# Seventeen gathered tiles and two fetched, fetches six blocks ahead, tokens scaled by ScalarE

## The chip, the cores and the metric

The kernel runs on one core of one Trainium2 chip. The metric is the time of one execution in device microseconds, as the median of several runs.

## The reference

A graph of N = 10000 nodes with 160000 edges (src, dst, both drawn at random) carries a 128-wide feature row per node. Seven hops each multiply the features by the normalized adjacency matrix; the eight stages of a node are its tokens, over which a small attention block and a readout run.

```python
h = x                                   # (10000, 128) f32
toks = [x]
for _ in range(7):
    msg = h[src] * deg_inv_sqrt[src, None] * deg_inv_sqrt[dst, None]
    h = segment_sum(msg, dst, N)
    toks.append(h)
tok = stack(toks, axis=1)               # (N, 8, D)
# layernorm, one self-attention over the 8 tokens, residual,
# layernorm, softmax readout over the 8 tokens -> (N, D)
```

## The kernel before

**Tables.** The features of a hop stand in SBUF as a table `tab` of 79 blocks of 128 nodes, 256 f16 wide: 128 columns of the rounded value and 128 of what rounding left over. A copy lies in DRAM (`tabd`), and of its last blocks, from block 4 * NG on, a second copy (`tabh`).

**Slots.** Source and destination blocks are paired. For each of the 78 full destination blocks (NW) and each source block there are 32 slots (CAP) for edges. Four source blocks share a *slot tile* of 128 slots. NG = 18 such tiles are *gathered*: four matmuls with a one-hot matrix of 128 x 32 each (`w`, its second part, fp8) bring the source rows of 4 x 32 slots from `tab` into a PSUM tile `p` (two slot tiles to a buffer, six buffers), ScalarE or VectorE copies `p` to an f16 tile `eb`, and one matmul with a one-hot matrix of 128 x 128 (`w`, its first part) scatters the slots to the 128 destinations in `acc`. The sources from block 72 on are cut into four cells by the constant CELL, which share NI = 1 slot tile that is *fetched*: an indirect DMA issued by GpSimd brings its 128 rows from `tabh` into a tile `og`, and one matmul scatters them. Edges that found no slot go into one more fetched tile, the *over* tile, from `tabd`, with its one-hot matrix `Sov`. The last, partial block is done apart (`ogt`, `end_block`).

**Closing a block.** VectorE adds the two halves of `acc` to `s`; `next_rows` scales `s` into the next table and stores it to `tabd` (and `tabh`) by SP's queue; `token_out` scales `s` into `r`, on GpSimd, and stores it by SP's queue to `tok`.

**Stages.** Pass A sorts the edges (to about 411 us). Hop 1 runs beside the building of the matrices `w`, for four blocks at a time (`place`, `left_out`, `matrices`), and each `w` goes to DRAM (`gsd`). The framework orders the instructions there. Hops 2 to 7 (`later`, `one`) are in an order written by hand: the blocks from 4 * NG on come first, then the others; SP loads `w` some three blocks ahead into five buffers. Within a block PE runs all its gathers, then the fetched tiles, then the scatters but for the last two pairs, which run after the gathers of the next block (`lag`). The close of a hop's first block is held back to the end of the second, and its over tile comes last, as does that of the second block, because over tiles may name any row and so wait for the whole table of the hop before.

**Fetches.** In hops 2 to 7 `ahead(k, n, ...)` runs behind the first eviction of block n and issues the fetches of block n + 2. `mark` first has GpSimd copy one or two columns of the new `eb` into the `og` tile. GpSimd's queue is in order, so all its later work stands behind that eviction.

Of the kernel before, what the change touches and what calls it, by code (L numbers as in the profile page):

```python
# [22 lines left out]
NG = 18  # L23
NI = 1
CELL = 334
# [5 lines left out]
CAP = 32  # L31
NJ = NG + NI
NS = 4 * NJ
# [4 lines left out]
NE = 3  # L38
BIG = 32768.0
# [4 lines left out]
class Hops:  # L44
    def __init__(self, ctx, dp, missing, tab1, tc, x, src, dst, dis):
# [37 lines left out]
        self.zero16 = cp.tile([128, 512], F16, name="zero16")  # L83
# [33 lines left out]
        self.held = []  # L117
# [111 lines left out]
    def lag(self, ep, pp, key, w, a, m):  # L229
# [5 lines left out]
        for b, r, e in parts:  # L235
            T.matmul(W[:, b, :(e - r) * m], self.id16, self.zero16[:, :(e - r) * m], start=True, stop=False, skip_group_check=True)
# [8 lines left out]
    def lag_rows(self, ep, pp, key, w, m):  # L245
# [6 lines left out]
        for b, r, e in parts:  # L252
            T.matmul(W[:, b, :e - r], self.id16, self.zero16[:, :e - r], start=True, stop=False, skip_group_check=True)
# [344 lines left out]
    def mark(self, o, after):  # L598

        if after is not None:  # L600
            self.nc.gpsimd.tensor_copy(o, after.to_broadcast(list(o.shape)))  # L601

    def fetch_end(self, k, src, after=None):
        self.mark(self.ogt[:, k, 0:1], after)
# [3 lines left out]
    def end_block(self, first, fin):  # L608
        m = 257 if first else 256
        acc = self.pacc.tile([128, 512], F32, name="acc", tag="acc")  # L610
        for k in range(NE):
            self.nc.tensor.matmul(acc[:, :m], self.Sov[:, NW + k, :], self.ogt[:, k, :m], start=k == 0, stop=k == NE - 1)
# [7 lines left out]
    def block(self, t, w, tab, og, pend, lag, runs, first, evac, fin, lead=False, late=False, mid=None, ahead=None):  # L620

        nc, V, A, T, G = self.nc, self.nc.vector, self.nc.scalar, self.nc.tensor, self.nc.gpsimd
        m = 257 if first else 256
        acc = []


        def fetched(i, start=False, stop=False):
            W = w[:, (NG + i) * 128:(NG + i + 1) * 128] if i < NI else self.Sov[:, t, :]  # L630
            T.matmul(acc[0][:, :256], W, og()[i], start=start, stop=stop)
            if first:
                T.matmul(acc[0][:, 256:257], W, self.ones16, start=False, stop=False)

        def begin():
            acc.append(self.pacc.tile([128, 512], F32, name="acc", tag="acc"))
            for i in range(NI if late else NI + 1):
                fetched(i, start=i == 0)

        def scat(e, jj):  # L640
            if not acc:
                acc.append(self.pacc.tile([128, 512], F32, name="acc", tag="acc"))
            for j in range(e.shape[1]):
                J = 2 * jj + j
                T.matmul(acc[0][:, :m], w[:, J * 128:(J + 1) * 128], e[:, j, :m], start=first and J == 0,  # L645
                         stop=J == NG - 1 and not (first or late))
                if first and J == 0 and not lead:
# [3 lines left out]
        def close():  # L651
            if first:
                if lead:
                    for i in range(NI):
                        fetched(i)
                T.matmul(acc[0][:, 256:257], self.Sov[:, t, :], self.ones16, start=False, stop=False)
            if first or late:
                T.matmul(acc[0][:, :256], self.Sov[:, t, :], og()[NI], start=False, stop=True)  # L658
            self.finish(t, acc[0], fin)

        def gather(jj):
            n = min(2, NG - 2 * jj)
            p = self.pg.tile([128, 2, 2, 128], F32, name="p")
            for j in range(n):
                for q in range(4):
                    s = 4 * (2 * jj + j) + q
# [847 lines left out]
```

## Time and profile before

| | us |
|---|---|
| runs | 3860.93, 3868.25, 3875.58 |
| median | 3868.25 |
| profiled execution, own time | 3870.73 |
| its span, first to last instruction | 3868.9 |
| pass A and decode | 0 to about 411 |
| hop 1 with the matrices | about 427 to 1117 |
| hops 2 to 7 | 1125 to 3187, each 342 to 345 |
| attention and readout | 3187 to 3869 |

In the profile a line such as "L897 PE MATMUL p<-tab,w ... x33696 | 1008.7, 273" gives line, engine, operation, the tile written and those read, the count, the busy time in us and the mean of one in ns; what follows the second bar is the engine's idle time just before and what ended it. PE is TensorE's matmuls, PEld its weight loads, DVE VectorE, ACT ScalarE, POOL GpSimd, SP the engine whose queue issues plain DMAs. Matmuls overlap, so the spacing of their starts tells more than the duration of one.

### The profile page before, as it was taken

To read this page: it belongs to the slowest core of one execution; us is meant where nothing else is said; L and a number is where in the kernel's file an instruction comes from. 1 tells how busy PE (TensorE), PEld (TensorE's weight loads), DVE (VectorE), ACT (ScalarE), POOL (GpSimd) and SP (SyncE) were. 2 spreads that over 40 slices of the span, in tenths; PEclk is the share of its full clock that TensorE was granted. 3 is DMA by queue.
4 is the path that set the end of the run, shared out by engine and by line. 5 is a ranking of instruction groups with operands and counts; after the bars stand their busy time and mean duration, and the time that the engine had idled before them with its cause. 6 is when DMAs were issued, how large, how long until landed. Compare 5 with 4: busy or idle time off the path is not lost.

```text
span 3868.9 us, 165983 instructions
## 1 busy us (share of the span) xinstructions
PE 3608.5 (93%) x69042; PEld 3019.7 (78%) x69042; DVE 2995.5 (77%) x6973; ACT 2743.1 (71%) x6934; POOL 1844.0 (48%) x2493
## 2 busy tenths in 40 slices
PE   5776899999979999999999999999999999999996
PEld 4665677777768888888888888888888887888885
DVE  8999898888867766766666766676665557999998
ACT  6775477777746666666666666666666669888884
POOL 0000254444446666666666666666666652222222
PEclk8888999999989999999999999999999999999998
DMA  2100354455546666666666666676677541222220
GB/s 91 50 1 1 124 185 163 166 175 177 172 138 207 202 201 202 204 200 200 206 202 204 201 204 201 199 207 202 201 212 212 186 160 48 76 76 76 76 76 24
DMA packets 320888, 590.64 MB, mean 153 GB/s; under 512 B 56780, under 2 KB 214698, under 8 KB 314874
## 3 DMA queue, kind: packets, MB, share of 16 engines
q1 hardware_dynamic: 281945, 501.79, 41.1%
q0 software_dynamic: 35616, 73.01, 7.9%
q8 instruction: 542, 8.88, 0.9%
q10 hardware_dynamic: 2560, 5.12, 0.5%
q14 instruction: 225, 1.84, 0.1%
HBM read 451.66 MB, written 128.06 MB: 150 GB/s over the span
## 4 chain that ended last, share of the span: by engine, by line
PE 71%; DVE 13%; issue 7%; POOL 4%; DMA 3%; ACT 2%; SPq 0%; POOLq 0%; DVEq 0%; ACTq 0%
PE p L897 20%; PE acc L885 19%; PE pv L1174 4%; PE po L1185 3%; PE pu L1163 3%; PE acc L880 3%; POOL og L591 2%; PE acc L645 2%; PE ta L341 2%; PE p L667 2%; PE pt L1153 2%; PE tm L420 2%; POOL r L703 1%; DVE ro L337 1%; DVE R L210 1%
## 5 line engine op out<-in xcount | busy, mean ns | idle before, releaser
L902 ACT CAST eb<-p 128x512 f16<-128x512 f32 x2808 | 1420.4, 602 | 649.4 <-PE p L897 646.3
L902 DVE CAST eb<-p 128x512 f16<-128x512 f32 x1404 | 946.4, 688 | 625.5 <-PE p L897 624.4
L897 PE MATMUL p<-tab,w 128*32 128x256 f16 x33696 | 1008.7, 273 | 5.4 <-DMA w<-gsd 4.6
L885 PE MATMUL acc<-eb,w 128*128 128x256 f16 x8424 | 997.7, 273 | 0.0
L897 PEld LDWEIGHTS <-w 128*32 128x32 fp8e3 x33696 | 859.8, 96 | 121.1 <-DMA tabd<-tab 61.9
L885 PEld LDWEIGHTS <-w 128*128 128x128 fp8e4 x8424 | 824.2, 98 | 96.9 <-issue 1.5
L591 POOL DMA_INDIRECT og<-tabh,oidx x546 | 604.3, 1107 | 386.6 <-POOL og L601 218.2
L591 POOL DMA_INDIRECT og<-tabd,oidx x546 | 563.6, 1032 | 288.9 <-PE acc L658 95.3
L703 POOL TENSOR_SCALAR r<-s,ctok 128x128 f32<-128x128 f32 x553 | 374.0, 676 | 172.3 <-DVE s L617 112.7
L670 ACT CAST eb<-p 128x512 f16<-128x512 f32 x686 | 357.4, 605 | 38.8 <-PE p L667 33.7
L327 ACT ACTIVATE o<-oh,d2s 128x79 f16<-128x79 f16 x800 | 204.6, 372 | 79.2 <-PE ta L341 79.2
L1199 ACT ACTIVATE junk<-tab 128x128 f32<-128x128 f32 x625 | 245.0, 394 | 0.1
L667 PE MATMUL p<-tab,w 128*32 128x256 f16 x5616 | 221.1, 275 | 23.4 <-ACT eb L670 15.0
L601 POOL COPY og<-eb 128x2 f16<-128x2 f16 (+1 forms) x494 | 94.8, 192 | 296.4 <-ACT eb L902 295.8
L795 DVE TENSOR_REDUCE s<-acc 128x128 f32<-128x256 f32 x468 | 194.6, 416 | 31.4 <-PE acc L885 16.0
L645 PE MATMUL acc<-eb,w 128*128 128x257 f16 x1404 | 198.3, 276 | 0.0
L1257 POOL TENSOR_TENSOR p<-e,in 128x512 f32<-128x512 f32 (+1 forms) x40 | 40.8, 1021 | 326.6 <-DVE e L1255 303.8
L341 PE MATMUL ta<-o,ro 128*128 128x158 f16 x1250 | 121.5, 270 | 77.1 <-DVE ro L337 77.1
L1185 PEld LDWEIGHTS po<-v,pT 128*128 128x128 f32 x1250 | 160.2, 194 | 41.4 <-issue 27.9
L667 PEld LDWEIGHTS <-w 128*32 128x32 fp8e3 x5616 | 136.1, 96 | 61.1 <-issue 45.2
L341 PEld LDWEIGHTS <-ro 128*128 128x128 f16 x1250 | 116.5, 115 | 81.3 <-DVE ro L337 81.3
L697 DVE SCALAR_TENSOR_TENSOR tab<-s,c,tab 128x128 f16<-128x128 f32 x474 | 168.3, 355 | 14.7
(330 smaller groups left out, 5386.0 us busy)
## 6 DMA issues: line engine op xcount, KB each, us to landing
w<-gsd SPq DMA_DIRECT2D x468, 592.0 KB
gsd<-w SPq DMA_DIRECT2D x78, 592.0 KB
rb<-srow SPq DMA_DIRECT2D x78, 576.0 KB
tok<-r SPq DMA_DIRECT2D x546, 64.0 KB
tab<-tok SPq DMA_DIRECT2D x273, 128.0 KB
tabd<-tab SPq DMA_DIRECT2D x474, 64.0 KB
og<-tabh,oidx POOLq DMA_INDIRECT x546
og<-tabd,oidx POOLq DMA_INDIRECT x546
```

What stands on the lines that cost most here:

```text
L327: A.activation(o[:, j - a, NK:, i], oh[:, j, :, i], AF.Copy, scale=d2s[:, c0:c0 + 1])
L341: T.matmul(ta, ro[:, j - a, :, i], o[:, j - a, :, i], start=j + i == 0, stop=j + i == NP)
L591: self.nc.gpsimd.indirect_dma_start(out=o, out_offset=None, in_=src[0] if i == NI else src[1], in_offset=bass.IndirectOffsetOnAxis(ap=self ...
L645: T.matmul(acc[0][:, :m], w[:, J * 128:(J + 1) * 128], e[:, j, :m], start=first and J == 0, stop=J == NG - 1 and not (first or late))
L667: T.matmul(p[32 * q:32 * q + 32, j], w[:, NJ * 128 + s * CAP:NJ * 128 + (s + 1) * CAP].bitcast(F8G), tab[:, s, :], start=True, stop=True)
L670: (A.copy if evac(jj) else V.tensor_copy)(e[:, :n, 0:256], p[:, :n].rearrange("p j h d -> p j (h d)"))
L703: self.nc.gpsimd.tensor_scalar(r, s, ct[:, t:t + 1], None, op0=ALU.mult)
L885: T.matmul(acc[0][:, :256], w[:, J * 128:(J + 1) * 128], e[:, j, 0:256], start=False, stop=J == NG - 1 and not late)
L897: T.matmul(p[32 * q:32 * q + 32, j], w[:, NJ * 128 + s * CAP:NJ * 128 + (s + 1) * CAP].bitcast(F8G), tab[:, s, :], start=True, stop=True)
L902: (A.copy if act else V.tensor_copy)(e[:, :, 0:256], p.rearrange("p j h d -> p j (h d)"))
L1185: T.matmul(p[:, g - a, :], PT[i % 2][:, g, :], S[i]["v"][:, g, :128], start=True, stop=True)
L1199: A.activation(j, S[i]["x"][:, g, :], AF.Square, bias=S[i]["x"][:, g, 0:1], scale=-1.0, accum_out=S[i]["sq"][:, g:g + 1])
```

## The change

- **Slots.** NG goes from 18 to 17 and NI from 1 to 2. A block has 68 gathers, 17 scatters, two fetched cell tiles and the over tile. Fetched sources begin at block 68 and have eight cells; `w` shrinks from 4736 to 4608 columns. The ninth `p` of a block holds one slot tile. NJ = NG + NI stays 19, and with it the work of `place`.
- **Fetches in hops 2 to 7.** `ahead` stands at the end of block n and issues the cell and over fetches of block n + 6; `og` has six buffers for seven. `mark` is gone. At a hop's end the cells of the next hop's first six blocks are fetched, and their over tiles in a row at its block 0.
- **Tokens in hops 2 to 7.** `token_out` runs on ScalarE, ahead of the next block's first eviction (in a hop's first block after the fourth pair).
- **Tidying.** Constants of zeros are one column read by broadcast; unused branches of `block` are gone; `gather` is shared by hop 1 and the later hops; hop 1 starts with quads 68-69, 70-73, 74-77 (before 72-73, 74-77). There are 21 quads in both.

```diff
-NG = 18
-NI = 1
-CELL = 334
+NG = 17
+NI = 2
+CELL = 404
...
+PAIRS = (NG + 1) // 2
+AHEAD = 6
...
-    def mark(self, o, after):
-        if after is not None:
-            self.nc.gpsimd.tensor_copy(o, after.to_broadcast(list(o.shape)))
...
+    def gather(self, w, tab, jj, pg, act):
+        n = min(2, NG - 2 * jj)
+        p = pg.tile([128, 2, 2, 128], F32, name="p")
+        for j in range(n):
+            for q in range(4):
+                ...
+        e = self.ebuf[self.eb_i % len(self.ebuf)]
+        self.eb_i += 1
+        (self.nc.scalar.copy if act else self.nc.vector.tensor_copy)(e[:, :n, 0:256], p[:, :n].rearrange("p j h d -> p j (h d)"))
+        return e[:, :n]
...
-    def token_out(self, k, t, s, ct):
+    def token_out(self, k, t, s, ct, act=False):
         r = self.fp.tile([128, 128], F32, name="r")
-        self.nc.gpsimd.tensor_scalar(r, s, ct[:, t:t + 1], None, op0=ALU.mult)
+        if act:
+            self.nc.scalar.activation(r, s, AF.Copy, scale=ct[:, t:t + 1])
+        else:
+            self.nc.gpsimd.tensor_scalar(r, s, ct[:, t:t + 1], None, op0=ALU.mult)
...
-        self.token_out(k, t, s, ct)
+        self.scaled.append(lambda: self.token_out(k, t, s, ct, True))
...
-            self.ogp = c.enter_context(tc.tile_pool(name="og2", bufs=7))
+            self.ogp = c.enter_context(tc.tile_pool(name="og2", bufs=AHEAD))
...
-        def pair(k, m, after, both=True):
+        def cells(k, m):
             o = self.ogp.tile([128, NI + 1, 256], F16, name="og")
             ogs[k][m] = [o[:, j, :] for j in range(NI + 1)]
-            self.mark(o[:, 0:2 if both else 1, 0:1], after)
-            self.rows_of(order[m], 0, dins[k % 2], o[:, 0, :])
-            if both:
-                self.rows_of(order[m], NI, dins[k % 2], o[:, NI, :])
+            for j in range(NI):
+                self.rows_of(order[m], j, dins[k % 2], o[:, j, :])
...
+        def over(k, m):
+            self.rows_of(order[m], NI, dins[k % 2], ogs[k][m][NI])
+
+        def ahead(k, n):
+            if n == 0:
+                for m in range(AHEAD):
+                    over(k, m)
+            m = n + AHEAD
+            if m < NW:
+                cells(k, m)
+                over(k, m)
+            elif k < nhop:
+                cells(k + 1, m - NW)
...
+            if not lead:
+                scaled()
+            for jj in range(PAIRS):
+                e = self.gather(w, tab, jj, self.pg, jj in (0, 1, 2, 3, 6, 8) if lead else jj % 3 != 1)
                 pend.append(lambda e=e, jj=jj: scat(e, jj))
-                if jj == 0:
-                    ahead(k, n, e[:, 0, 0:1])
                 if jj == 4:
                     advance()
+                if lead and jj == 3:
+                    scaled()
...
             (held if lead else pend).append(close)
+            ahead(k, n)
-        for m in range(4):
-            pair(2, m, None, False)
+        for m in range(AHEAD):
+            cells(2, m)
```

GpSimd's queue at the start of hop 2, before. `tabh` rows are cell fetches, `tabd` rows over fetches, COPY rows the marks, `r` the token's scaling:

```order
L591 DMA og<-tabh_149,oidx 128x256 x4
L601 COPY og<-eb_251 128x1
L591 DMA og<-tabh_149,oidx 128x256
L601 COPY og<-eb_251 128x1
L591 DMA og<-tabd_147,oidx 128x256
L601 COPY og<-eb_22634 128x1
L591 DMA og<-tabd_147,oidx 128x256
L601 COPY og<-eb_22634 128x1
L591 DMA og<-tabd_147,oidx 128x256
L703 TENSOR_SCALAR r<-s,ctok_243 128x128
```

The same place now:

```order
L592 DMA og<-tabh_149,oidx 128x256 x12
L592 DMA og<-tabd_147,oidx 128x256 x6
L592 DMA og<-tabh_149,oidx 128x256 x2
L592 DMA og<-tabd_147,oidx 128x256
L592 DMA og<-tabh_149,oidx 128x256 x2
```

Twelve cell fetches in place of five stand ahead of the first over fetch, and from then on each block has two cell fetches and one over fetch with neither mark nor scaling between them.

ScalarE's queue in the middle of a later hop, now (L664 is the eviction of a pair of slot tiles, 128x256 that of the single last one; before, the queue held six evictions of 128x2x256 a block, L902, and nothing else):

```order
L677 ACTIVATE r<-s,ctok_244 128x128
L664 CAST eb_22558<-p 128x2x256
L664 CAST eb_22560<-p 128x2x256
L664 CAST eb_22561<-p 128x2x256
L664 CAST eb_22563<-p 128x2x256
L664 CAST eb_22564<-p 128x2x256
L664 CAST eb_253<-p 128x256
L677 ACTIVATE r<-s,ctok_244 128x128
```

The scaling stands ahead of the first eviction of each block, and one eviction is half as wide.

SP's queue at the end of hop 2 and the start of hop 3, before (`tok` is the store of a token, `tabd` that of a table row block, `w` a load):

```order
L705 DMA tok_151<-r 128x128
L166 DMA tabd_146<-tab_239 128x256
L705 DMA tok_151<-r 128x128
L166 DMA tabd_146<-tab_239 128x256
L836 DMA w<-gsd_143 128x4736
L836 DMA w<-gsd_144 128x4736
L836 DMA w<-gsd_145 128x4736
```

And now:

```order
L681 DMA tok_151<-r 128x128
L167 DMA tabd_146<-tab_239 128x256 x3
L681 DMA tok_151<-r 128x128 x2
L812 DMA w<-gsd_139 128x4608
L812 DMA w<-gsd_140 128x4608
L812 DMA w<-gsd_141 128x4608
```

The last two token stores moved behind the last table store, and the three loads of `w` stand behind them as before.

More of the change, by code (lines that the diff above doesn't have):

```diff
@@ L651, in close @@
         def close():
[L652 to L658, printed above, removed]
[L659 to L671 removed]
+            if lead:
+                for i in range(NI):
+                    fetched(i)
```

112 lines of the change are left out of this document (34 added, 78 removed).

## The prediction

> **What bounds the kernel now.** I read the page's first part, the busy table by stage, the merged timeline of TensorE in one block of a hop, and last the groups of what waits.
>
> ```profile
> PE 3608.5 (93%) x69042; PEld 3019.7 (78%) x69042; DVE 2995.5 (77%) x6973; ACT 2743.1 (71%) x6934; POOL 1844.0 (48%) x2493
> 427.00:1117.00 690.00, 629.52 (x12084) 508.14 (x12082) 596.07 (x1185) 493.00 (x1081) 325.75 (x239) 0.98 0.50 165
> ...
> 1813.40:2157.00 343.60, 341.87 (x7181) 289.74 (x7181) 238.53 (x563) 236.72 (x468) 222.17 (x325) 1.00 0.69 202
> ```
>
> Columns of a stage: length, busy PE, weight load, DVE, ACT, POOL, granted clock, DMA share, GB/s. The second row is hop 1, the third hop 4, which stands for the six later hops: PE is busy in 341.87 of 343.60 us at full clock, and beside its own weight loads nothing is above 70%.
>
> ```profile
> 1598.96 2.15 PE L897 MATMUL p<-tab,w 128*32 128x256 f16 x72
> 1601.04 0.28 PE L880 MATMUL acc<-og,w 128*128 128x256 f16 x1
> 1601.16 0.27 PE L880 MATMUL acc<-og,Sov 128*128 128x256 f16 x1
> 1601.27 2.13 PE L885 MATMUL acc<-eb,w 128*128 128x256 f16 x18
> 1603.33 2.15 PE L897 MATMUL p<-tab,w 128*32 128x256 f16 x72
> L902 ACT CAST eb<-p 128x512 f16<-128x512 f32 x464 | 234.8, 602 | 107.1 <-PE p L897 107.1
> L902 DVE CAST eb<-p 128x512 f16<-128x512 f32 x232 | 156.7, 688 | 98.7 <-PE p L897 98.7
> L880 PE MATMUL acc<-og,Sov 128*128 128x256 f16 x77 | 21.0, 273 | 1.7 <-DMA og<-tabd,oidx 1.7
> ```
>
> From start to start a block is 4.37 us without a gap: 72 gathers in 2.08 (28.9 ns each), two fetched tiles in 0.23 (0.115 each), 18 scatters in 2.06 (0.115 each). The three groups (of 1470 to 1810) say who waits: both evacuating engines wait for PE's gathers, over 1.2 us a block, while PE waits 1.7 us in a whole hop. So PE issue is the bound here, and what is taken off PE comes off the span until something else catches up.
>
> **The change part by part, hops 2 to 7 first.**
>
> *17 gathered tiles, 2 fetched.* Per block PE loses four gathers (4 x 28.9 = 0.116 us) and one scatter (0.115), and gains one fetched matmul (0.115). Over 6 x 78 = 468 blocks the net is 468 x 0.116 = **-54 us**. The period becomes about 4.255 us. What could eat this is whoever must now keep that period:
>
> ```profile
> L591 POOL DMA_INDIRECT og<-tabh,oidx x76 | 77.5, 1020 | 39.1 <-POOL og L601 35.2 <-issue 3.1 <-DMA w<-gsd 0.8
> L591 POOL DMA_INDIRECT og<-tabd,oidx x78 | 74.3, 953 | 27.7 <-DMA w<-gsd 16.2 <-issue 10.7 <-POOL og L601 0.8
> L703 POOL TENSOR_SCALAR r<-s,ctok 128x128 f32<-128x128 f32 x78 | 48.9, 626 | 3.6 <-DVE s L795 1.1
> 1118.94 1.00 POOL L591 DMA_INDIRECT og<-tabh,oidx  x1 [0.68 <-issue]
> 1120.26 0.95 POOL L591 DMA_INDIRECT og<-tabh,oidx  x1 [0.30 <-issue]
> 1128.72 0.98 POOL L591 DMA_INDIRECT og<-tabd,oidx  x1 [0.27 <-POOL og L601]
> 1599.90 2.54 ACT L902 CAST eb<-p 128x512 f16<-128x512 f32 x5
> 1602.34 0.41 DVE L795 TENSOR_REDUCE s<-acc 128x128 f32<-128x256 f32 x1
> 1603.78 2.54 ACT L902 CAST eb<-p 128x512 f16<-128x512 f32 x5 [1.33 <-PE p L897]
> L183 ACT ACTIVATE tab<-tab,disT 128x128 f32<-128x128 f32 x79 | 23.3, 386 | 7.6 <-DVE esel L386 7.6
> q0 software_dynamic: 35616, 73.01, 7.9%
> og<-tabh,oidx POOLq DMA_INDIRECT x546
> og<-tabd,oidx POOLq DMA_INDIRECT x546
> ```
>
> *POOL.* The scaling (0.63) and the marks leave, a third fetch comes: 3 x (1.0 + 0.30 between two) = 3.9 us of 4.255. That is 92%, tight but under, and the only thing left on POOL there. A late fetch costs PE nothing until it is six blocks late (25 us). I take 0.
>
> *ACT.* It gets a scaling, priced by the like activation in pass A, 0.386 us, and loses half an eviction. The place matters: it stands before a block's first eviction and waits for DVE's sum `s`. That sum ends at 1602.34 + 0.41 = 1602.75; ACT has been idle since 1599.90 + 2.54 = 1602.44 and has its next eviction only at 1603.78. Even with gathers 0.116 us shorter the scaling (to about 1603.15) fits. 0; without that gap it would be 0.39 us a block.
>
> *DMA.* Of the software queue the row gives packets, MB and the share of sixteen engines' span. One issue takes 0.079 x 3868.9 x 16 engines / 1113 issues (these 1092, and 21 of the end block) = 4.4 engine-us, 0.275 us of all sixteen. A block has 0.69 x 4.37 = 3.0 us now, less 0.05 for the smaller `w`, plus 0.275: 3.24 of 4.255, or 76%. The next `w` is asked for over three blocks ahead. 0.
>
> *The marks go.* They held POOL, not PE (PE's wait above), so nothing comes off the path. The fetch of block n+6 now waits for PE to have used block n's buffer, which is a pace of one block per block as well.
>
> *Hop starts.* Two small terms:
>
> ```profile
> 1134.75 0.27 PE L880 MATMUL acc<-og,Sov 128*128 128x256 f16 x1
> 1818.78 0.97 POOL L591 DMA_INDIRECT og<-tabd,oidx  x1 [2.33 <-DMA tabd<-tab]
> 1821.68 0.97 POOL L591 DMA_INDIRECT og<-tabd,oidx  x1 [0.27 <-POOL og L601]
> 1823.09 0.28 PE L880 MATMUL acc<-og,Sov 128*128 128x256 f16 x1 [0.95 <-DMA og<-tabd,oidx]
> 1826.43 0.28 PE L880 MATMUL acc<-og,Sov 128*128 128x256 f16 x1 [0.55 <-DMA og<-tabd,oidx]
> 1814.84 0.32 SPq L705 DMA_DIRECT2D tok<-r  x1
> 1815.27 1.14 SPq L166 DMA_DIRECT2D tabd<-tab  x1
> ```
>
> Hop 2: twelve cell fetches (before: four, then one) now stand ahead of the first over fetch. At 1.25 us each from 1118.94 it is issued from 1134.0 to 1135.0 instead of at 1128.72. PE wants it at about 1134.5. If it landed at once, PE would wait 0.5 us; with the 3.3 us between the end of an issue and PE's use at a later boundary (1819.75 to 1823.09, beside three `w` loads) 3.8, and the third over fetch may add 0.5. I take **+3.3 us**, near the boundary's row, since the first `w` loads are over by then. Hops 3 to 7: the over fetches wait for the last `tabd` write. On SP that write stood behind the last token's store, which waited for POOL; the store now follows it, some 0.4 us earlier. The third over fetch is also spared two marks. PE's two waits of 0.95 and 0.55 us shrink by some 0.4 us: 5 x -0.4 = **-2 us**. The six over fetches in a row beside three `w` loads could as well cost that: -4 to +5.
>
> **Hop 1.** The second and third rows are of the list of waits (us in total, times, longest), the last two are pieces of the chain that ended last.
>
> ```profile
> L591 POOL DMA_INDIRECT og<-tabh,oidx x76 | 124.5, 1638 | 110.6 <-PE acc L631 98.7 <-issue 5.3 <-PE acc L658 3.8
> POOL og L591 <- PE acc L631: 99.3, 55, 12.0
> PE acc L658 <- DMA og<-tabd,oidx: 4.6, 2, 3.8
> L582 DVE TENSOR_SCALAR w<-rb,pid 128x2304 fp8e3<-128x2304 f16 x39 | 55.1, 1413 | 7.8 <-DMA rb<-srow 4.3 <-PE acc L656 3.4
> 605.48 0.99 PE p L667 x32
> 606.47 0.99 PE acc L645 x8
> ```
>
> PE and DVE take turns (630 and 596 of 690 us busy). PE saves four gathers at 31 ns, 0.124 us a block; scatter against fetched tile cancels. DVE's `gw` shrinks by 1/18, 78 ns on every second block. On the path all the time that is 78 x (0.124 + 0.039) = 12.7 us; since they take turns I take 40%, **-5 us**. The other end is POOL: a third fetch costs 1.64 + 0.3 us here. POOL is idle 364 / 78 = 4.7 us a block, so it has room, but if the wait that comes with it falls on the path for a fifth of the blocks it is 78 x 1.94 / 5 = +30.
>
> The Trainium skill (SBUF — State Buffer, "SBUF: two separate sides") speaks against this part: while DVE runs a two-port operation GpSimd is locked out and cannot write the descriptors of a DMA it issues. The trace agrees: the same fetch takes 1638 ns in hop 1, with its large f16 operations on DVE, and 1020 ns in the later hops. By that rule a third fetch is dearest in hop 1; by the rows POOL still has 4.7 us of idle time there, so the sum stays at -5.
>
> *The rest.* The constant of zeros read by broadcast, the cells' constant, other quads (21 as before) and four more `tabh` stores a hop on SP: 0, SP waits most of the time. Attention is unchanged; the token rows that it loads ahead are of blocks finished at least two blocks earlier.
>
> **Sum:** -54 - 5 + 3.3 - 2 = -58 against the profiled execution's 3870.73 gives 3813. That execution is 2.5 us above the median of 3868.25, so I say **3811 us**, 1.5% less.
>
> **Rivals.**
>
> *POOL becomes the bound (slower).* If the fetches in hops 2 to 7 cost as in hop 1, 3 x (1.64 + 0.3) = 5.8 us against 4.255, POOL would set the period after the lead of six blocks is used up: 468 x (5.8 - 4.37) = +670 us. At 1.2 us a fetch (4.5 a block) it is +60 us, 3930. It decides from 1.16 us a fetch with its gap of 0.30 (4.37 a block). For it: 92% filled. Against: 76 and 78 fetches of a hop averaged 1020 and 953, and DVE's work in the block stays the same. 7%.
>
> *Hop 1 takes it back.* The +30 above and the two hop-start terms at their worst: -54 + 30 + 9 = -15, 3853, within 0.5%. For it: POOL's waits of up to 12.0 us for buffers there, with more now queued behind them; against: PE waited for a fetch twice in that hop, 4.6 us in all. 4%.
>
> *PE is not the bound after all.* The Trainium skill (Perfetto Trace Analysis, "Identifying the Most-Contended Engine") says that matmul busy time flatters PE and that weight-load busy time is the better measure of headroom. That is 289.74 of 343.60 us, 84%. Read as 16% of slack, 0.7 us a block would swallow the 0.116, and the time stays at 3868. As a mechanism of this kernel: a drain or switch between the 32-column and the 128-column matmuls would set the period, and it stays. Against it: four gathers take the time of one scatter (2.08 us for 72, 2.06 for 18), so nothing is left over for a switch, and the engines around wait for PE. 3%.
>
> *More comes off.* If hop 1 gives all 12.7 us and the hop starts cost nothing: -70, 3798.
>
> **Chances and range.** My forecast with its neighbours (3796 to 3838) 83%; further off but still faster by over 0.5% 3%; no change (within 0.5%, about what a measurement of this kernel can tell) 7%; slower 7%, nearly all POOL. The range takes in the end of 3798 and two thirds of the way from 3811 to the hop-1 rival's 3853.
>
> **What would show it.** Right: hops 2 to 7 at 332 to 336 us each (343.6 now), PE still over 99% busy, blocks of 68 gathers in 1.97 us; POOL some 87 to 92% busy there; a wait of about 3 us before the first over tile of hop 2; ACT's scaling between the last eviction of one block and the first of the next. Wrong: PE waiting for `og` in mid-hop, ACT's first eviction late behind the scaling, or hop 1 longer than 690 us.

## The result and the profile after

The changed kernel took 3841.44 us (median of 6 runs, 3837.15 to 3849.4) beside 3867.64 us for the kernel before on the same chip: a ratio of 0.9934, 95% interval 0.9918 to 0.9951. It is faster by 26 us; forecast were 57, and 3841 lies above the forecast range. The profiled execution took 3838.73 us, 32.0 less than that of before. And this holds for one chip. On the chips that the experiments ran on, the same kernel was 22 and 23% slower than before, and every variant of it was slower too. What sets those runs apart is called the chip here; no run returned to the first one, so the chip, its machine and the hour are not separated. The two misses, of the forecast and of the sign, have different causes, and both are taken up below.

The page of the changed kernel, its busy row, and then the stages hop 1 and hops 2 to 4 (columns as in the prediction):

```profile
PE 3551.1 (93%) x66936; PEld 2963.4 (77%) x66936; DVE 2994.4 (78%) x6973; ACT 2810.2 (73%) x7408; POOL 1955.1 (51%) x2053
```
```profile
427.00:1119.00 692.00, 622.21 (x11863) 505.48 (x11860) 595.45 (x1187) 471.55 (x1081) 423.74 (x315) 0.98 0.52 167
1127.26:1477.74 350.48, 340.28 (x6880) 285.49 (x6880) 241.85 (x582) 250.34 (x545) 230.96 (x248) 0.98 0.71 214
1477.74:1816.29 338.55, 335.33 (x6872) 282.54 (x6871) 239.07 (x563) 251.86 (x547) 223.79 (x238) 0.99 0.73 217
1816.29:2151.11 334.82, 333.63 (x6872) 281.69 (x6871) 239.69 (x563) 251.35 (x547) 224.05 (x238) 1.00 0.75 220
```

Hop 4 is what was forecast (332 to 336), and hops 5 and 6 take 335.5 and 334.9. Hops 2 and 3 are not: 350.5 and 338.6 us, with 10.2 and 3.2 us in which TensorE does nothing. The same stages of the kernel before:

```profile
1125.22:1469.59 344.37, 344.24 (x7192) 292.16 (x7192) 241.64 (x582) 236.81 (x468) 221.96 (x326) 1.00 0.69 205
1469.59:1813.41 343.82, 342.05 (x7183) 289.96 (x7182) 239.21 (x564) 236.71 (x468) 222.51 (x325) 1.00 0.68 202
```

Stage by stage, from the first gathers of each hop in both traces, after minus before: up to hop 1 +1.4 us, hop 1 +0.7, hop 2 +6.1, hop 3 -5.3, hop 4 -9.1, hop 5 -8.6, hop 6 -9.1, hop 7 -8.1, attention +0.1: together -32.0 before rounding.

**Hop 2 lost 8.3 us in one block.** The blocks on both sides of block 11 take 4.26 us, block 11 takes 12.54. The timeline of all engines there (start, length, engine, line, operation, idle time before it and what ended it):

```profile
1177.80 0.94 POOL L600 DMA_INDIRECT ogt<-tabd,oidx  x1 [0.30 <-issue]
1179.05 0.95 POOL L592 DMA_INDIRECT og<-tabh,oidx  x1 [0.30 <-PE acc L858]
1180.30 1.49 PE L660 MATMUL p<-tab,w 128*32 128x256 f16 x48
...
1185.29 0.94 POOL L592 DMA_INDIRECT og<-tabd,oidx  x1 [0.30 <-issue]
1186.24 0.27 POOL L1005 IOTA aip<- 128x128 int32 x1
1186.54 0.23 DVE L1007 TENSOR_SCALAR aident<-aip 128x128 f32<-128x128 int32 x1 [7.04 <-POOL aip L1005]
1186.95 0.42 DVE L771 TENSOR_REDUCE s<-acc 128x128 f32<-128x256 f32 x1
1187.40 0.40 ACT L677 ACTIVATE r<-s,ctok 128x128 f32<-128x128 f32 x1 [8.08 <-DVE s L771]
1187.71 2.79 ACT L664 CAST eb<-p 128x512 f16<-128x512 f32 x6
1188.32 1.26 PE L660 MATMUL p<-tab,w 128*32 128x256 f16 x20 [6.53 <-ACT eb L664]
1190.12 2.78 PE L858 MATMUL acc<-eb,w 128*128 128x256 f16 x17
1192.83 2.04 PE L660 MATMUL p<-tab,w 128*32 128x256 f16 x68
```

Block 11 begins with the gathers at 1180.30, block 12 with those at 1192.83.

Read from the bottom: TensorE waits 6.53 us for an eviction; ScalarE, which owes it, stands in its queue behind the scaling `r` and waits 8.08 us for VectorE's `s`; VectorE waits 7.04 us for `aip`, the first tile of the attention constants, which `beside` builds after block 10 of hop 2 (lines 1001 to 1011); and that IOTA of 0.27 us stands in GpSimd's queue behind the six fetches from 1179.05 on. GpSimd is still nearly two blocks behind after the twelve cell and six over fetches of the start: at 1177.80, in block 10, it issues the end block's fetch that `ahead` puts behind block 8. VectorE's own evictions stand behind the same wait and start at 1187.28, so TensorE would have stalled without the scaling too: by these starts the scaling adds some 0.6 us (an estimate), not the stall. Then the 17 scatters take 2.78 us instead of 2.02: the granted clock is 0.50 from 1184.9 to 1191.6. In the kernel before, VectorE waits 0.94 us for the same tile:

```profile
1174.67 0.23 DVE L1039 TENSOR_SCALAR aident<-aip 128x128 f32<-128x128 int32 x1 [0.94 <-POOL aip L1037]
```

**The start of hop 2** lost another 4.5 us: blocks 1 and 2 take 7.63 and 5.99 us (4.67 and 4.53 before).

```profile
1139.82 0.27 PE L853 MATMUL acc<-og,Sov 128*128 128x256 f16 x1 [2.80 <-DMA og<-tabd,oidx]
1140.24 3.65 PE L660 MATMUL p<-tab,w 128*32 128x256 f16 x68
```
```profile
1140.00:1145.00 5.00, 5.00 (x82) 3.64 (x81) 3.34 (x8) 3.39 (x7) 3.78 (x4) 0.66 0.29 71
```

The forecast wait is there (2.80 us), and behind it something that was not forecast: 68 gathers take 3.65 us instead of 2.04, under a granted clock of 0.66 (the last row, with columns as above). At hop 3 a wait of 2.22 us is followed by 3.29 us for the 68; at hop 4 one of 0.88 us by the usual 2.05.

**Hop 1** has one long wait, where the longest of its kind was 3.8 us before:

```profile
509.39 0.37 PE L638 MATMUL acc<-og,Sov 128*128 128x256 f16 x1 [10.33 <-DMA og<-tabd,oidx]
```
```profile
494.88 1.01 POOL L592 DMA_INDIRECT og<-tabh,oidx  x1 [0.16 <-PE tm L474]
496.19 6.45 POOL L592 DMA_INDIRECT og<-tabh,oidx  x1 [0.30 <-issue]
502.94 1.09 POOL L592 DMA_INDIRECT og<-tabd,oidx  x1 [0.30 <-issue]
```

The over fetch (`tabd`) stands behind two cell fetches, and the second of these takes 6.45 us. Slow fetches are not new: the longest two of the kernel before took 5.81 and 5.58 us, at 498 and 463 us in hop 1. While the one of 6.45 us runs, VectorE works without a gap, mostly on large f16 operations (496.37 to 503.21).

### The profile page after: what moved, and what is told of

Same layout as the page of the kernel before. It is cut to its first block, busy times and chain, and to the rows that moved or that the text cites. A ratio compares the mean times of both kernels' runs of the same rounds, so it can differ in the third digit from the quotient of the medians.

```text
span 3836.9 us, 160416 instructions
## 1 busy us (share of the span) xinstructions
PE 3551.1 (93%) x66936; PEld 2963.4 (77%) x66936; DVE 2994.4 (78%) x6973; ACT 2810.2 (73%) x7408; POOL 1955.1 (51%) x2053
## 4 chain that ended last, share of the span: by engine, by line
PE 62%; DVE 4%; DMA 2%; ACT 1%; issue 1%; POOL 0%; DVEq 0%; POOLq 0%; ACTq 0%
PE p L660 23%; PE acc L858 22%; PE acc L853 5%; PE pv L1142 3%; PE po L1153 3%; PE pu L1131 3%; PE pt L1121 2%; PE ps L1173 1%; DMA og<-tabd,oidx 1%; PE pf L1321 1%; DVE st L1248 1%; PE sm L1179 1%; DVE o L1159 1%; ACT junk L1167 1%; POOL og L592 0%
## 5 line engine op out<-in xcount | busy, mean ns | idle before, releaser
L664 ACT CAST eb<-p 128x512 f16<-128x512 f32 (+1 forms) x3494 | 1662.6, 570 | 331.8 <-PE p L660 318.0
L592 POOL DMA_INDIRECT og<-tabh,oidx x1092 | 1132.4, 1037 | 658.6 <-PE acc L853 313.0
L664 DVE CAST eb<-p 128x512 f16<-128x512 f32 x1420 | 955.9, 687 | 590.8 <-PE p L660 588.7
L660 PE MATMUL p<-tab,w 128*32 128x256 f16 x37128 | 1172.3, 274 | 32.9 <-ACT eb L664 18.7
L660 PEld LDWEIGHTS <-w 128*32 128x32 fp8e3 x37128 | 943.0, 97 | 204.9 <-issue 101.1
L858 PE MATMUL acc<-eb,w 128*128 128x256 f16 x7956 | 947.6, 273 | 0.0
L858 PEld LDWEIGHTS <-w 128*128 128x128 fp8e4 x7956 | 779.0, 98 | 101.3 <-issue 10.9
L677 ACT ACTIVATE r<-s,ctok 128x128 f32<-128x128 f32 x474 | 189.9, 402 | 253.4 <-DVE s L771 247.1
L853 PE MATMUL acc<-og,w 128*128 128x256 f16 x936 | 183.5, 278 | 0.8 <-DMA og<-tabh,oidx 0.8
L1142 PE MATMUL pv<-Wv,xT 128*128 128x131 f32 x1250 | 175.1, 282 | 3.8 <-ACT xT L1122 1.8
L1153 PE MATMUL po<-v,pT 128*128 128x128 f32 x1250 | 166.8, 277 | 7.0 <-DVE o L1159 5.4
```

What stands on the lines that cost most here:

```text
L592: self.nc.gpsimd.indirect_dma_start(out=o, out_offset=None, in_=src[0] if i == NI else src[1], in_offset=bass.IndirectOffsetOnAxis(ap=self ...
L660: self.nc.tensor.matmul(p[32 * q:32 * q + 32, j], w[:, NJ * 128 + s * CAP:NJ * 128 + (s + 1) * CAP].bitcast(F8G), tab[:, s, :], start=True ...
L664: (self.nc.scalar.copy if act else self.nc.vector.tensor_copy)(e[:, :n, 0:256], p[:, :n].rearrange("p j h d -> p j (h d)"))
L853: T.matmul(acc[0][:, :256], W, og[n][i], start=start, stop=stop)
L858: T.matmul(acc[0][:, :256], w[:, J * 128:(J + 1) * 128], e[:, j, 0:256], start=False, stop=J == NG - 1 and not late)
L1142: T.matmul(p[:, g - a, :], S[i]["xT"][:, g, :], Wv, start=True, stop=True)
```

## Experiments

The first four runs met another chip: the kernel before took 3911 us there, and every variant of the changed kernel some 4800. So the later runs ask first what that is. The edits are to the changed kernel unless another is named; ratios are to the kernel before on the same chip.

**e1: read the IOTA later.**

```
         G.iota(ip, ...)
+        pr = ...; G.iota(pr, ...)      # moved up
+        yield                          # five blocks on
         V.tensor_scalar(ident, ip, ...)
```

> The changed kernel, with one thing moved: the two IOTAs of the attention constants are still issued after block 10 of hop 2, but VectorE reads them only after block 15. Theory (GpSimd's queue): after block 10 VectorE waited 7.0 us for an IOTA that stood behind GpSimd's backlog of fetches; ScalarE's scaling waited for VectorE, the next evictions stood behind it, and TensorE stalled 6.5 us and then ran at a lower clock. Then block 11 of hop 2 falls from 12.5 us to under 5, hop 2 from 350.5 to about 342.5 us, and the kernel is 8 us faster than the changed one, about 0.991 of before. Rival 1 (the stall is of the fetches or of DMA, and the IOTA only stands beside it): block 11 keeps 10 us or more, no gain. Rival 2 (the wait moves): the same stall shows after block 15 or 16, no gain.

Measured: 4788.2 us, 1.2242 (1.2223 to 1.2261). VectorE's wait for the IOTA, 3.05 us in the changed kernel on such a chip, is gone (0.0), but TensorE is held up elsewhere in every block, so the price of that wait could not be read.

**e2: hop 2's over fetches block by block.**

```
+            if n == 0 and k > 2:       # was: n == 0
...
             cells(2, m)
+            over(2, m)
```

> The changed kernel, with hop 2's first six over fetches issued block by block with the cell fetches (two cells, one over, and so on) instead of behind all twelve cells. Theory: TensorE's wait of 2.8 us before the first over tile goes, and with it the lower clock behind it (0.66 granted in the 5 us after); blocks 1 and 2 of hop 2 fall from 7.63 and 5.99 us to under 5 each, 4 us in all. But GpSimd still needs the same 22 us for these 18 fetches and is then further behind TensorE, so VectorE's wait for the IOTA after block 10 grows by about as much (7 to about 11 us) and the kernel gains 0 to 1 us: hop 2 stays at 349 to 351 us. Rival (the two losses are independent): the wait for the IOTA stays at 7 us, hop 2 falls by 4 us to 346.5. Rival 2: the first over tile is late because of the load on DMA (share 1.01 at 1127 to 1131), not its place in the queue: the wait of 2 to 3 us stays.

Measured: 4780.9 us, 1.2226 (1.2208 to 1.2245). Inconclusive for the same reason.

**e3: a third over buffer in hop 1.**

```
+            self.ogo = tile_pool(name="og1o", bufs=3, ...)   # for i == NI; the cells keep bufs=2
```

> The changed kernel, with a third buffer for the over tile in hop 1 (cells keep two). In GpSimd's queue the over fetch of every fourth block then stands four cell fetches earlier. Theory: TensorE's 10.3 us wait in hop 1 came from an over fetch behind four cell fetches, one of which took 6.45 us; the wait goes to 4 us or less and hop 1 (start to hop 2's start, 709.1 us) shortens by 4 to 6 us. Rival (TensorE and VectorE take turns, and the wait is made up for later, or another wait takes its place): hop 1 stays within 1.5 us of 709.

Measured: 4805.62 us, 1.2292 (1.2269 to 1.2316). Hop 1 can be compared among these four runs: from its first gathers to the token factors of hop 2 it takes 722 us in e1 and 719 in e2 (703 on the first chip). Here it became 735 us, and the wait for the over tile stayed, at 10.5 us. My theory fell: the over fetch has one earlier place in the queue, but the fetch of 6.45 us is still ahead of it. What makes that one slow was not tried.

**e4: the three together.**

> The changed kernel with the three edits together. Theory: -8 (IOTA), -4 (hop 2's first over tiles, now without the loss that the IOTA made of it) and -4 to -6 (hop 1): 16 to 18 us below the changed kernel, about 3824 us, 0.989 of before; hop 2 at 338 us. Rival (the losses are taken up elsewhere): less than 9 us.

Measured: 4807.16 us, 1.2287 (1.227 to 1.2304). No answer on hop 2 either. Hop 1 took 741 us with the third buffer in it, so that buffer costs time there.

**c1 to c4: the chip, and the parts of the change one by one.**

> The changed kernel once more, as it is, since the four runs with small edits came to 4781 to 4807 us on another chip, where the kernel before takes 3911 us: blocks of hops 2 to 7 last 6.2 us there, with TensorE, VectorE and ScalarE all pausing in the gathers. If the chip decides (theory: this chip sets off in the changed kernel a stall that the first chip did not): about 4790 us on the same chip, 3840 on one like the first. If the edits did it (rival): about 3880 us even on that chip, 0.993 of before.

> The kernel before, as it is, for its profile on the same chip. Theory: 0.998 to 1.002 of before; where the chip is like the second, its blocks are nearer 4.4 than 4.37 us, and the same pauses of all three engines show, smaller. Rival: no such pauses at all, so that the changed kernel alone sets them off.

The third: the new tiling with the old look-ahead and GpSimd's scaling, that is, `pair`, `over`, `ahead` and `mark` of the kernel before with two cells in a pair.

> The changed tiling alone: 17 gathered and two fetched tiles, but with the kernel before's look-ahead (a pair two blocks ahead, with marks that hold the fetches back) and the tokens scaled on GpSimd. Theory: GpSimd then has three fetches (3.75 us), a scaling (0.63) and a mark or more a block, 4.5 us or more against 4.26: it becomes the bound, blocks of 4.5 to 4.8 us, the kernel 3900 to 4050 us. Rival (GpSimd still keeps up): blocks of 4.26 us and 3815 to 3840 us. Where blocks of the changed kernel take 6.2 us, blocks near 6.2 us here say that the third fetch sets off the stall, and not the look-ahead or the scaling.

The fourth: `NG = 18`, `NI = 1` and the old cell constant and quads, all else as changed.

> The rest alone: 18 gathered tiles and one fetched as before, but six blocks ahead without marks and tokens scaled on ScalarE. Theory: blocks stay at 4.37 us; with two fetches a block GpSimd is soon through its backlog, so VectorE hardly waits for the IOTA in hop 2, and hop starts are as before or up to 2 us better: 3850 to 3872 us. Rival (the look-ahead itself costs): the same two stalls in hop 2 as in the changed kernel, 8 to 12 us, 3875 to 3885 us. Where blocks of the changed kernel take 6.2 us, blocks of 4.4 us here leave the third fetch and the tiling as the cause.

Measured: c1 4779.77 us, 1.2228 (1.2208 to 1.2248); c2 3912.07, 1.0004 (0.9994 to 1.0014); c3 4509.88, 1.1537 (1.1518 to 1.1556); c4 4196.88, 1.0736 (1.0718 to 1.0754). The edits of e1 to e4 were not it: the changed kernel as it is takes as long there (c1). And both halves of the change cost time there (c3, c4). c1, 400 us of the middle hops, with a row of TensorE's list of waits and one of ScalarE's (us, times, longest):

```profile
2000.00:2400.00 400.00, 327.29 (x5530) 230.76 (x5518) 191.32 (x457) 208.56 (x442) 180.41 (x192) 0.98 0.51 149
```
```profile
PE p L660 <- issue: 57.4, 112, 1.1
ACT eb L664 <- PE p L660: 135.9, 114, 2.4
```

No engine is full: TensorE, busy for 327 us by the page, does 5530 matmuls in the 400 us (8198 on the first chip), and GpSimd is at 45%. ScalarE waits for TensorE, and TensorE for nothing that the profile shows. The timeline of one block of c1 shows what goes on at these times:

```profile
2005.19 0.95 POOL L592 DMA_INDIRECT og<-tabh,oidx  x1 [0.31 <-issue]
2005.46 1.62 PE L660 MATMUL p<-tab,w 128*32 128x256 f16 x44
2006.03 0.59 ACT L664 CAST eb<-p 128x512 f16<-128x512 f32 x1 [0.62 <-PE p L660]
2006.44 0.95 POOL L592 DMA_INDIRECT og<-tabd,oidx  x1 [0.30 <-issue]
2008.15 0.54 PE L660 MATMUL p<-tab,w 128*32 128x256 f16 x11 [0.42 <-issue]
2008.25 1.29 DVE L664 CAST eb<-p 128x512 f16<-128x512 f32 x2 [3.27 <-PE p L660]
```

44 gathers are recorded by 2007.1, yet VectorE, whose first eviction needs only the second eight of them, starts at 2008.25, 0.86 us after GpSimd's issue ended at 2007.39. At the start of hop 2, where GpSimd issues 18 in a row, it is worst: 68 gathers take 20 us, in pieces, and VectorE waits 23 us for the second eight.

```profile
1143.86 3.29 PE L660 MATMUL p<-tab,w 128*32 128x256 f16 x48 [4.44 <-DMA w<-gsd]
...
1163.66 0.41 PE L660 MATMUL p<-tab,w 128*32 128x256 f16 x2 [1.70 <-issue]
1163.76 1.29 DVE L664 CAST eb<-p 128x512 f16<-128x512 f32 x2 [23.12 <-remote]
```

In the kernel before, on such a chip (c2), a block's two fetches stand otherwise, the first at the end of the gathers and the second among the scatters, and the next gathers lose nothing:

```profile
2000.33 2.15 PE L897 MATMUL p<-tab,w 128*32 128x256 f16 x72
2002.17 1.02 POOL L591 DMA_INDIRECT og<-tabh,oidx  x1 [0.29 <-POOL og L601]
2002.64 2.13 PE L885 MATMUL acc<-eb,w 128*128 128x256 f16 x18
2003.50 0.95 POOL L591 DMA_INDIRECT og<-tabd,oidx  x1 [0.31 <-issue]
2004.69 2.15 PE L897 MATMUL p<-tab,w 128*32 128x256 f16 x72
```

In one of its slow blocks (5.66 us; 4.37 is the rule there too) a third fetch, for the end block, falls on the gathers:

```profile
2221.59 0.72 PE L897 MATMUL p<-tab,w 128*32 128x256 f16 x17
2221.80 0.98 POOL L605 DMA_INDIRECT ogt<-tabd,oidx  x1 [0.27 <-issue]
2223.34 1.69 PE L897 MATMUL p<-tab,w 128*32 128x256 f16 x51 [0.43 <-issue]
```

So I took, for every block after 1400 us, the time from the end of the matmul that carries the first signal of the gathers to ScalarE's first eviction, by what GpSimd did at that end (medians, worked out from the traces; in brackets the blocks):

```
                        indirect DMA being issued   none for 0.6 us
before, first chip              52 ns  (26)             52 ns (354)
after,  first chip              52 ns (375)             52 ns   (6)
c2 (before)                   1504 ns  (18)             91 ns (291)
c1 (after)                     852 ns (416)             51 ns   (5)
c4 (rest alone)                781 ns (377)             51 ns  (38)
c3 (slots alone)              1626 ns (382)             52 ns  (19)
d3 (late marks)                 51 ns (389)             51 ns   (6)
f2 (third plain)                52 ns (347)             52 ns  (57)
```

In c1 to c4 this signal of TensorE arrives late while GpSimd issues an indirect DMA, on the first chip never. The last two rows are of runs told below, and they bound the rule: there the first signal comes on time under an issue, and the next is the late one (VectorE's first eviction, behind the second eight gathers: 1085 ns in d3 and 321 in f2, 121 on the first chip). So not every signal that falls into an issue is held, and which are is open. The ends of matmuls are modelled, so a late signal cannot be told from a matmul that ends late. Other engines' signals do not: from VectorE's `s` to ScalarE's `r` it takes 35 ns on the first chip and 34 in c1, from `r` to SyncE's store 26 and 26, issue or not.

**d1 to d4: is it GpSimd's issue, or the load of `w` that fills the DMA engines at the same time?** d1 loads five `w` tiles in hops 2 to 7 and goes on with those, so later blocks multiply with other blocks' matrices; d2 leaves the second cell's fetch out and multiplies the first cell's rows in its place; d3 is the kernel before with one number changed, so that the marks wait for the seventh eviction of a block; d4 weaves gathers and scatters.

```
d1:  +            if t is not None and len(once) < 5:      # then w = once[... % 5]
d2:  -            for j in range(NI):
d2:  +            self.rows_of(order[m], 0, ...)
d3:  -                if jj == 0:                          # of the kernel before
d3:  +                if jj == 6:
d3:                       ahead(k, n, e[:, 0, 0:1])
d4:  +                while len(pend) > lag:               # lag = 4, after each pair
d4:  +                    pend.pop(0)()
```

> The changed kernel without its loads of w in hops 2 to 7 beyond the first five blocks: later blocks multiply with one of those five tiles (left out: 463 loads; the sums are those of other tiles). On a chip where the changed kernel's blocks take 6.2 us: theory 1 (GpSimd's indirect DMAs hold up what TensorE signals to the evacuating engines, and it costs where they meet the gathers): the blocks stay at 5.8 us or more, the kernel over 4550 us. Theory 2 (the w load, which fills all 16 DMA engines during the gathers, stalls them): blocks of 4.26 us, the kernel near 3850 us. On a chip like the first: 4.26 us, about 3835 us, by both.

> The changed kernel with its second cell fetch left out in hops 2 to 7 (the first cell's rows are multiplied in its place). Theory 1: with two fetches a block, not held, only the end of the second meets the gathers: blocks of 4.7 to 4.9 us on a chip where three fetches make 6.2, the kernel 4050 to 4170 us. Theory 2: blocks stay above 5.8 us. On a chip like the first: 4.26 us; with GpSimd soon through its backlog the IOTA is hardly waited for (hop 2 near 340 us instead of 350): about 3830 us.

> The kernel before with one thing changed: the marks wait for the seventh eviction of a block instead of the first, so that the same two fetches are issued about 2 us later, the second one during the next block's gathers. Theory 1: on a chip like the second, a block goes from 4.37 to 5.2 to 5.7 us (as blocks 9, 13 and 17 do there, in which the end block's fetch falls on the gathers), the kernel to 4300 to 4500 us. Theory 2 (w): no change, below 3930 us. On a chip like the first: 4.37 us and no change, by both.

> The changed kernel with gathers and scatters woven in hops 2 to 7: after each pair of gathered tiles one pair is scattered, four pairs behind, instead of all gathers first; an accumulator's sum is taken as soon as it is closed. Theory 1: the six PSUM buffers then cover 6 x 0.46 = 2.8 us of late signals instead of 1.4, so on a chip where the changed kernel's blocks take 6.2 us they fall to 4.4 to 5.2, the kernel to 3900 to 4300 us. Theory 2: still over 5.5 us. On a chip like the first: 4.26 us a block and a shorter wait at the hop starts, since the closing of the first blocks comes later: 3825 to 3840 us; if a switch between 32 and 128 columns costs anything, 18 switches a block show it: 4.3 us or more.

Measured: d1 4845.43 us, 1.2336 (1.2308 to 1.2365), blocks of 6.35 us: the load is not it. d2 4228.4, 1.0763 (1.0738 to 1.0788), 4.98 us. d3 4507.71, 1.1473 (1.1446 to 1.15), 5.74 us: nothing but the place of the marks, and with it the time of the two fetches, was moved, and it costs 1.37 us a block. That bears out theory 1 as far as the place of the fetches goes. One block of d3, in which the first eviction (ScalarE) is on time and the second (VectorE) is late:

```profile
2001.14 1.02 POOL L591 DMA_INDIRECT og<-tabh,oidx  x1 [0.51 <-POOL og L601]
2001.59 2.01 PE L897 MATMUL p<-tab,w 128*32 128x256 f16 x51
2002.04 0.59 ACT L902 CAST eb<-p 128x512 f16<-128x512 f32 x1 [1.17 <-PE p L897]
2003.29 0.69 DVE L902 CAST eb<-p 128x512 f16<-128x512 f32 x1 [2.37 <-PE p L897]
```

d4 5342.48, 1.36 (1.3562 to 1.3637), some 7.4 us a block: a miss. Weaving needs a signal for every pair, so, as I read it, each late signal now stops TensorE. And where nothing waits, eight gathers and two scatters take 0.66 us (start to start) where the prediction's averages give 0.46:

```profile
2006.94 0.40 PE L660 MATMUL p<-tab,w 128*32 128x256 f16 x8
2007.60 0.40 PE L660 MATMUL p<-tab,w 128*32 128x256 f16 x8
```

That is a switch between the two kinds, and it is in every trace: between 1500 and 3000 us the starts of two scatters stand 109 ns apart, those of a scatter and the next gather 202 or 203, those of a gather and the next fetched tile 205 (medians, before and after alike). Four gathers take 108 ns, of which the step to the next four is 99. A switch thus costs some 100 ns, two of them 0.2 us a block, and 18 of them in d4 1.8 us (estimates from these spacings).

**f1 to f4: the issue or the transfer, any DMA or the indirect one, and which half of the rest.** f1 and f2 bring the second cell tile as 128 consecutive rows of the table, not the rows that the edges name; f3 is the kernel before with `token_out` on ScalarE; f4 is e1 and e2 in one.

```
f1:  +            nc.sync.dma_start(o[:, 1, :], tabd rows)
f2:  +            nc.gpsimd.dma_start(o[:, 1, :], tabd rows)
f3:  +            self.nc.scalar.activation(r, s, AF.Copy, scale=ct[:, t:t + 1])
```

> The changed kernel, in which the second cell tile of hops 2 to 7 is not gathered by GpSimd but brought by SyncE as 128 consecutive rows of the table (other rows than the reference's). The bytes and the wait stay, GpSimd issues two DMAs a block. Theory 1a (what holds up TensorE's signals is GpSimd's issuing): on a chip where the changed kernel's blocks take 6.2 us, 4.8 to 5.1 us, as with the fetch left out. Theory 1b (the transfer itself does it): 5.8 us or more. On a chip like the first 4.26 us by both.

> The same with the 128 consecutive rows brought by a plain DMA that GpSimd issues. If any DMA that GpSimd issues holds the signals up: 5.6 to 6.3 us a block on a chip where the changed kernel's take 6.2. If only the indirect one does: 4.8 to 5.1 us.

> The kernel before with the tokens scaled on ScalarE alone (18 and one tiles, marks and two blocks ahead as before). Theory: the marks keep both issues between the gathers, so a block stays at 4.37 us on any chip, and the kernel within 0.4% of before; the 0.57 us a block of the rest alone were the look-ahead without marks. Rival (the scaling in front of the first eviction costs): 4.5 to 4.9 us a block.

> The changed kernel with VectorE reading the IOTA five blocks later and hop 2's over fetches issued block by block. On a chip like the first: hop 2 from 350.5 to about 338 us and the kernel about 12 us below the changed one, near 3828 us. On a chip where the changed kernel's blocks take 6.2 us: no difference from it, since GpSimd has no backlog there.

Measured: f1 4252.76 us, 1.0816 (1.0798 to 1.0834), 5.02 us a block, as with the fetch left out (4.98 in d2): the bytes, brought by SyncE as consecutive rows, cost next to nothing. f2 4165.47, 1.0603 (1.0585 to 1.062), 4.87 us: a plain DMA of GpSimd's costs nothing (4.98 with the fetch left out), the indirect one does. Whether it is the issuing of an indirect fetch or the transfer of its scattered rows behind it, these runs do not separate. f2's own block shows both kinds, the plain one at L830 and the one indirect fetch that meets the gathers:

```profile
2002.78 0.59 POOL L830 DMA_DIRECT2D og<-tabd  x1
2003.35 2.65 PE L660 MATMUL p<-tab,w 128*32 128x256 f16 x68
2003.67 0.98 POOL L592 DMA_INDIRECT og<-tabd,oidx  x1 [0.30 <-issue]
2005.08 2.33 ACT L664 CAST eb<-p 128x512 f16<-128x512 f32 x5 [0.68 <-PE p L660]
```

One such fetch makes 68 gathers last 2.65 instead of 2.04 us. f3 3960.76, 1.0084 (1.0067 to 1.0101): its block is 4.37 us as expected, which leaves the look-ahead without marks as what costs c4 its 0.57 us a block; but 31 us are lost in single blocks that I did not trace further, so the expectation of 0.4% failed. f4 4845.62, 1.2333 (1.2313 to 1.2354), no answer.

**g1, g2: once more, for a chip like the first.**

> The changed kernel with VectorE reading the IOTA five blocks later and hop 2's over fetches issued block by block, once more on another chip. On a chip like the first (before at 3868 us): hop 2 at about 338 us and the kernel 10 to 12 us below the changed kernel beside it. On one like the other four: blocks of 6.2 to 6.4 us again and no difference.

> The changed kernel as it is, beside g1. On a chip like the first 0.993 of before with hop 2 at 350 us; on one like the other four 1.22 to 1.24 of before.

Measured: 4845.28 us, 1.2334 (1.2314 to 1.2355), and 4845.51, 1.2337 (1.2316 to 1.2357). Again a chip of the second kind, and no difference. The record numbers it like that of c1 to c4, where the changed kernel took 4780 us, so a chip's number does not fix the time either. No version beat the kernel before on these chips, and none of these runs met a chip like the first.

## Why the prediction was wrong

*What held, on the first chip.* The tiling term: blocks of 4.26 us (4.255 forecast), 68 gathers in 1.97, hops 4 to 6 shorter by 9.1, 8.6 and 9.1 us (54 / 6 = 9). ScalarE's scaling costs nothing: in hop 2 it runs at 1175.61 to 1176.01, before the next gathers at 1176.04. GpSimd keeps pace: 3 x 1.25 = 3.75 of 4.26 us, 88% (67% in hop 4's row, which leaves out the 0.30 us between two fetches). The 2.8 us wait at the start of hop 2 was forecast as about 3. TensorE is the bound there. One reading behind that was wrong, though: that "nothing is left over for a switch". The averages of 28.9 and 115 ns had two switches of some 100 ns a block in them; both kernels pay them alike, so the term came out.

*The step that failed* is "A late fetch costs PE nothing until it is six blocks late (25 us). I take 0", with the 0 of *The rest*. True of the fetches, but GpSimd's queue also carries the IOTAs of the constants, and the argument looked only at what was in the steady block. A backlog that no fetch feels is felt by the first other instruction in the queue whose result someone needs. VectorE needs it, and its evictions and the sum `s` wait with it; the scaling that the change put in front of ScalarE's evictions, rightly costed at 0 where `s` is on time, makes ScalarE wait as well. Both hold TensorE's buffers. Price: 12.54 - 4.26 = 8.3 us. This is read from the trace; the runs that should have shown it met the other kind of chip, so it is not shown by experiment.

*Mis-sized: hop starts.* +3.3 for hop 2 measured +4.5, and -0.4 for hop 3 measured +1.9 in its block 1 (7.43 instead of 5.52 us), because the waits of 2.80 and 2.22 us are paid twice, in the wait and in the clock behind it. *Hop 1:* -5 forecast, +0.7 measured. VectorE's `gw` did shrink (1413 to 1347 ns), TensorE's busy time too (629.5 to 622.2), but TensorE's longest wait for an over fetch grew from 3.8 to 10.3 us, and its waits for VectorE's `R` from 8.0 to 13.6 us in all. Which of these took the 5 us back is not shown: e3, which was to take the first away, failed. A further 1.4 us went before hop 1, where I had 0. Of the 25.7 us by which the sum missed the profiled execution (-57.7 and -32.0), hop 2 has 11.8, hop 1 5.7, hop 3 4.1, the stretch before hop 1 1.4, the other hops 2.6 and attention 0.1; another 6 us lie between the profiled executions and the medians. One sum of the rivals does not come out either: *More comes off* needs the -4 of the hop starts beside -54 and -12.7 to reach -70.

*On the later chips* the sign was wrong, and no rival had it. "POOL becomes the bound" is slower too, but GpSimd is at 45% there. The step is the sentence on the marks: "They held POOL, not PE (PE's wait above), so nothing comes off the path." They did hold GpSimd, and that was their use: in c2 the two fetches of a block are issued 1.84 and 3.17 us after its first gather, so that what they hold up falls on the end of the gathers and on the scatters. It is there (the ninth eviction starts 1.13 us behind its gathers in c2 and 0.71 in the first chip's trace, medians) and costs nothing: blocks stay at 4.37 us, since the scatters of the last two pairs run only behind the next gathers. Without marks, or with a third fetch, the fetches fall on the gathers. That their place is the cause is shown by d3, for this kind of chip; by what way an indirect fetch makes TensorE's signals late is not. In the first chip's trace of before nothing of it could be seen: there, signals take 52 ns either way.

## What to carry to other kernels

Before an engine is filled to 88% with work that has slack, list everything else in its queue and who waits for that; a one-time instruction behind a backlog can stop three engines. A hold that costs nothing in the trace may be there for when it issues, not for what it waits for: move it alone, as d3 does, before it is thrown out. And time a change on more than one chip: here the same pair of kernels gave 0.993 on one and 1.22 and 1.23 on others.

## What the runs showed of the hardware

On the later chips TensorE's first signal of a block came 781 to 1626 ns after the end that the profile gives for its matmul when GpSimd was issuing an indirect DMA (c1 to c4), on the first chip 52 ns. In d3 and f2 the first came after 51 and 52 ns in spite of an issue, and the second after 1085 and 321. Signals of VectorE and ScalarE stayed at 34 and 26 ns, and a plain DMA from GpSimd in place of an indirect one cost nothing (4.87 us a block in f2, 4.98 without it in d2). What differs between the chips, and where the signal is held, is open. The Trainium skill (SBUF — State Buffer, "Who interferes with whom") says of the ports into SBUF that TensorE and ScalarE never wait on anyone; no run here shows whether a port has a part in the late signals. The Trainium skill (Perfetto Trace Analysis, "Tensor Engine Instruction (MATMUL, LD_WEIGHTS)") says that the update is pushed only once PSUM has acknowledged the bytes, after the estimated end that the profile shows; that is the stretch in which the 852 ns lie, and no run here tells which part of it.

A switch between matmuls of 32 and of 128 columns cost some 100 ns (202 to 205 ns from start to start, 99 to 109 without it).

The granted clock fell after short waits: behind the one of 2.80 us it is 0.50 from 1140.5 to 1143.8 (0.66 over the 5 us of the row above), behind the one of 2.22 us 0.50 from 1488.7 to 1492.0, and behind the one of 0.88 us it stays at 1.00. The Trainium skill (TensorE: Matmul & The Clock Gate, "What's actually happening") puts the fall after an idle window of about 3.4 us that runs freely; waits of 2.80 and 2.22 us were enough here, so the measurement decides.
